# Attention scores in quarter products, gate products moved behind the values, and work exchanged between GpSimd and VectorE

## The chip, the cores and the metric

The kernel runs on one core of one Trainium2 chip. The metric is the device time of one execution in microseconds, the median of the runs. A core has five engines with queues of their own: TensorE (PE in the profile, with its weight loads as PEld), VectorE (DVE), ScalarE (ACT), GpSimd (POOL) and SyncE (SP), which here only issues transfers.

## What is computed

Attention over keys and values that are averaged in groups of eight, and behind it a layer of eight experts. A token takes part in the second if a score says so, and goes to one expert.

```python
# q, k, v: (8, 8, 576, 64); pool = 8, so Sp = 72
k_p = k.reshape(B, H, Sp, pool, D).mean(axis=3)
v_p = v.reshape(B, H, Sp, pool, D).mean(axis=3)
scores = scale * np.matmul(q, k_p.transpose(0, 1, 3, 2))
scores = scores - np.max(scores, axis=-1, keepdims=True)
attn = np.exp(scores)
attn = attn / (np.sum(attn, axis=-1, keepdims=True) + 1e-09)
x = matmul(attn, v_p), as 4608 tokens x 512
# experts
do_compute = x @ w_skip > 0
logits = x[do_compute] @ w_gate                  # 8 experts
e_idx, gate_w = argmax and its softmax weight
h = np.maximum(xc @ w1[e], 0.0)                  # 512 -> 1024
out[do_compute] = xc + gate_w * (h @ w2[e])      # 1024 -> 512; other rows are x itself
```

## The kernel before

Two halves follow each other: attention (`attention`, until about 147 us), then the experts (`experts`). Between them stands the work that turns the routing into lists of tokens (`slots`).

Attention goes over 36 tiles of 128 tokens. A batch has 576 tokens, four and a half tiles, so four tiles straddle two batches. Products on TensorE are fp32; a product of two fp32 operands shows in the profile as two records, each with a weight load. Heads are taken in pairs: `kbd` holds the summed keys of two heads as a block diagonal, 128 rows by 2 x 72 columns, and a query block of 128 rows (two heads of 64) by 128 tokens is the weight side. `scores` (L299) makes the scores of four heads into a bank `sc`, and is called twice for a tile. On a straddling tile each product is made twice, for 64 tokens each (`parts`, L294).

The steps of tile t in the loop from L842, in the order in which the program is written:

- `turned_p` (L326), ScalarE: copies the turned probabilities of tile t-2 out of `pt`, 640 columns in one instruction.
- `normal(t-3)` (L797), VectorE: divides the values of tile t-3 (`rc`, `l8`, `x`), issues the output write on SP, sums the gate logits `lg`, and takes up to two routing steps.
- `scores` of tile t, TensorE; `softmax`, VectorE: the minima `mn` (`least`, L307) of both halves.
- If a batch's gates are due: `gates_pe` (L275, TensorE) here, ahead of the values; `gates_dve` (L280, VectorE) behind the turns.
- `routes.products()`: the ranking products of a routing group (L397 to L401).
- `exponentials`, ScalarE: eight instructions (L315) of 72 columns.
- `values(t-2)` (L331), TensorE: six fp32 products into `o`.
- `turn_p` (L318), TensorE: five turns of tile t-1's exponentials into `pt`.
- VectorE's planned work (`dve.take`), more routing steps up to a budget, GpSimd's planned work (`gps.take`), and, one tile before a batch's gates, `turn_v` (L258).

GpSimd's work is planned by `Spaced` (L640): an item has a first tile, a last tile and a cost; items go in order of their last tile, and writes to the routing table (L415, one indirect DMA a tile) are put between them, at least 1.2 us of other work apart where there is other work. From tile 26 on (`FILLS`) a memset that clears a row block (L768) is put between two writes that have less than 0.5 us between them. Its items are: the sums of a batch's values over eight (`sums`, L241, four large and four small steps), the block-diagonal value operand (`values_both`, L269), the low parts of expert weights (`low`, L584), and the routing table's writes. Expert weights are split into a high part (ScalarE, L581) and a low part, weight minus high part. Of chunks 2 to 6 the second half's low part is made by VectorE (`low_v`, L588), the others by GpSimd; a chunk's place in `stage` is loaded again when both are made. SP issues loads and output writes in program order.

Behind the last tile TensorE works on 56 product steps of one expert (`tile_steps`), in a fixed order; 20 of them are left for the time after the hand-over to `experts`. In between `slots` has GpSimd gather rows of the routing table (L1040) once the last table write has landed, and TensorE turn them (L1072).

## Time and profile before

| | us |
|---|---|
| median of 3 runs | 480.49 |
| lowest and highest | 479.95 and 480.70 |
| profiled execution, its own time | 481.24 |
| its span in the profile | 479.2 |
| granted TensorE clock, mean of the span | 0.999 |

| engine | busy us of the span |
|---|---|
| TensorE (matmul records) | 463.5 (97%) |
| VectorE | 303.4 (63%) |
| GpSimd | 250.3 (52%) |
| ScalarE | 225.7 (47%) |

The shares are averages over two halves that are not alike: VectorE, ScalarE and GpSimd are much busier in the attention half. A busy TensorE is a chain of overlapping records, whose ends are modelled; distances between starts say more than the length of one.

### The profile page before, as it was taken

The numbers are of one execution on the slowest core, as the hardware profiler recorded it, in microseconds if no ns is written. First come the engines' busy times: TensorE is split into PE (matmuls) and PEld (weight loads), VectorE is DVE, ScalarE is ACT, GpSimd is POOL, SyncE is SP. The second block draws the span as 40 slices with busy tenths as digits, with TensorE's granted clock in tenths as the row PEclk, the third lists the DMA queues.
The fourth block names the chain that finished last, engine by engine and source line by source line (L and its number), as shares of the span: only waits on it lengthen the run. The fifth ranks groups of instructions, "written<-read, shape, count | busy, mean of one in ns | idle before, by whom it ended". The sixth has DMA issues, their size and how long they took to land. (4 is left out here: it accounts for less than half of the span.)

```text
span 479.2 us, 11182 instructions
## 1 busy us (share of the span) xinstructions
PE 463.5 (97%) x3043; PEld 417.1 (87%) x3044; DVE 303.4 (63%) x713; ACT 225.7 (47%) x578; POOL 250.3 (52%) x328
## 2 busy tenths in 40 slices
PE   7999999999999999899999999999999999999995
PEld 4799899989999979798989987989899898989894
DVE  5877888798788622578795667663846554343321
ACT  5678768888891211546462645612435251212110
POOL 4499499999998154363342424362624161515242
PEclk9999999999999999999999999999999999999999
DMA  8999999996931026679787497877687223322021
GB/s 278 388 396 390 361 352 332 384 333 207 328 122 68 11 62 215 230 228 308 247 289 244 136 290 241 300 240 251 202 256 262 89 95 101 129 66 88 22 88 42
DMA packets 52042, 103.88 MB, mean 217 GB/s; under 512 B 10031, under 2 KB 22959, under 8 KB 50336
## 3 DMA queue, kind: packets, MB, share of 16 engines
q1 hardware_dynamic: 40544, 78.18, 47.8%
q0 software_dynamic: 11456, 25.22, 15.0%
q8 instruction: 17, 0.28, 0.2%
q14 instruction: 25, 0.20, 0.1%
HBM read 80.85 MB, written 31.21 MB: 234 GB/s over the span
## 5 line engine op out<-in xcount | busy, mean ns | idle before, releaser
L1289 POOL DMA_INDIRECT out<-ring,slot x33 | 35.8, 1085 | 109.3 <-POOLq L1115 105.6
L315 ACT ACTIVATE e<-sc,mn 128x72 f32<-128x72 f32 x288 | 65.0, 345 | 7.4 <-DVE mn L309 6.8
L1527 ACT ACTIVATE hhi<-psl 128x256 fp32r<-128x256 f32 (+3 forms) x59 | 23.5, 400 | 94.0 <-ACTq L1115 93.5
L1384 PE MATMUL psl<-xlo,w1hi 128*128 128x256 f32 (+3 forms) x220 | 64.1, 291 | 0.0
L1383 PE MATMUL psl<-xhi,w1hi 128*128 128x256 f32 (+3 forms) x220 | 64.0, 291 | 0.0
L1385 PE MATMUL psl<-xhi,w1lo 128*128 128x256 f32 (+3 forms) x220 | 64.0, 291 | 0.0
L1284 POOL DMA_INDIRECT ring<-out,slot x42 | 46.6, 1109 | 22.6 <-issue 22.4
L341 PE MATMUL o<-vbd,pT 128*128 128x148 f32 (+1 forms) x312 | 49.4, 298 | 1.1 <-DVE x L360 1.1
L1626 DVE SCALAR_TENSOR_TENSOR hlo<-psl,hhi 128x256 fp32r<-128x256 f32 (+2 forms) x55 | 23.2, 423 | 41.3 <-DVEq L1115 39.0
L415 POOL DMA_INDIRECT table<-pay,r_di x36 | 36.7, 1018 | 12.6 <-DVE mb L443 6.4
L1383 PEld LDWEIGHTS psl<-xhi,w1hi 128*128 128x128 f32 x220 | 41.3, 188 | 0.8 <-issue 0.4
L1384 PEld LDWEIGHTS psl<-xlo,w1hi 128*128 128x128 f32 x220 | 41.3, 188 | 0.5
L341 PEld LDWEIGHTS o<-vbd,pT 128*128 128x128 f32 (+1 forms) x312 | 38.6, 179 | 3.6 <-ACT ring L213 1.0
L1385 PEld LDWEIGHTS psl<-xhi,w1lo 128*128 128x128 f32 x220 | 41.2, 187 | 0.0
L1297 POOL DMA_DIRECT2D sorted<-ring x39 | 22.2, 572 | 32.9 <-DMA ring<-out,slot 25.8
L1603 DVE TENSOR_TENSOR w2lo<-stage,w2hi 128x1024 fp32r<-128x1024 f32 x28 | 34.3, 1223 | 6.6 <-DVEq L1115 6.4
L1384 PE MATMUL psd<-xlo,w1hi 128*128 128x256 f32 (+3 forms) x132 | 38.4, 291 | 0.0
L1385 PE MATMUL psd<-xhi,w1lo 128*128 128x256 f32 (+3 forms) x132 | 38.4, 291 | 0.0
L1383 PE MATMUL psd<-xhi,w1hi 128*128 128x256 f32 (+3 forms) x132 | 38.4, 291 | 0.0
L1409 PE MATMUL mb<-w2hi,hlo 128*128 128x512 f32 x88 | 34.8, 396 | 0.0
L1409 PE MATMUL psf<-w2hi,hlo 128*128 128x512 f32 x88 | 34.8, 396 | 0.0
L1407 PE MATMUL psf<-w2hi,hhi 128*128 128x512 f32 x88 | 34.8, 395 | 0.0
(276 smaller groups left out, 1216.0 us busy)
## 6 DMA issues: line engine op xcount, KB each, us to landing
stage<-in_w SPq DMA_DIRECT2D x64, 512.0 KB, 5.5
sorted<-ring POOLq DMA_DIRECT2D x39, 256.0 KB, 3.3
out<-x SPq DMA_DIRECT2D x36, 256.0 KB, 5.4
stage<-in_k SPq DMA_DIRECT2D x6, 1152.0 KB, 8.8
blocks<-sorted SPq DMA_DIRECT2D x100, 64.0 KB
qt<-in_q SPq DMA_DIRECT2D x9, 512.0 KB, 7.4
hhi<-in_vm SPq DMA_DIRECT2D x4, 1024.0 KB, 7.7
hlo<-in_vm SPq DMA_DIRECT2D x3, 1024.0 KB, 9.8
```

The costliest lines, as they stand in the source:

```text
L315: nc.scalar.activation(ev[:, h // 2, k0:k0 + SP], sc[:, h * SP:(h + 1) * SP], AF.Exp, bias=mn[:, 4 * i + h:4 * i + h + 1], scale=-1.0)
L341: nc.tensor.matmul(o_[sl, g * 2 * VA:(g + 1) * 2 * VA], pT[:, 2 * a + g, sl], vbd[b % 2][:, 2 * a + g, :], start=(g == 0), stop=False)
L415: m = nc.gpsimd.indirect_dma_start(table, bass.IndirectOffsetOnAxis(ap=di[:, j:j + 1], axis=0), flat(fin["pays"][:, t0 + j:t0 + j + TW // ...
L1284: g.indirect_dma_start(ring[:, (s + 3) % 9, 0:D], None, out, bass.IndirectOffsetOnAxis(ap=slot[:, s:s + 1], axis=0), bounds_check=NTOK - 1 ...
L1289: g.indirect_dma_start(out, bass.IndirectOffsetOnAxis(ap=offsets, axis=0), ring[:, (s + 3) % 9, 0:D], None, bounds_check=NTOK - 1, oob_is_ ...
L1383: t.matmul(ps, whi[0][:, k, w], xhi[:, k, xs], start=(k == 0), stop=False)
L1384: t.matmul(ps, whi[0][:, k, w], xlo[:, k, xs], start=False, stop=False)
L1385: last = t.matmul(ps, wlo[0][:, k, w], xhi[:, k, xs], start=False, stop=(k == 3))
L1407: t.matmul(ps, hhi[:, k, sl], whi[1][:, k, :], start=(k == 0), stop=False)
L1409: last = t.matmul(ps, hlo[:, k, sl], whi[1][:, k, :], start=False, stop=(k == 7))
L1527: a.activation(hhi[:, f, xs], bank(f, xs, alone), AF.Relu).then_inc(sem["act"], 1)
L1603: v.tensor_tensor(chunk_of(wlo, c), chunk_view(stage[c], c), chunk_of(whi, c).bitcast(F32), ALU.subtract).then_inc(sem["wlo1" if c < 4 els ...
```

## The change

It does these things:

- From tile 3 on a tile's scores are made in quarters: 64 rows (one head) by 64 tokens, 72 columns, with head parity choosing the bank. The first three tiles stay as they were (`scores_by_halves`). `exped` takes its columns from the banks accordingly.
- The turned probabilities lie in two banks of `pt` (three turns in the first, two in the second), and two copies instead of one take them out. The turned value sums move within `pt`.
- `gates_pe` is written behind the values of its tile; `gates_dve` goes to the next tile, ahead of that tile's scores.
- Routing products that were not yet due when the tile began go behind the values from tile 15 on; after such products a tile takes one more routing step. The two steps for the gate weight come before the two for the rank.
- All low parts of chunks 0 to 6 are planned on GpSimd; chunk 7's stay on VectorE.
- For batches 3, 5 and 7 GpSimd makes two of the four large steps of the value sums, and VectorE sums the four parts that are left in one reduction, ahead of the minima of the tile before the batch's gates. The value operand of these batches may start two tiles later and ends one tile later.

```diff
+FOURS = 3, 5, 7
@@ sums
-            if b:
+            if b and b not in FOURS:
                 first += [add(vt[:, 0:2], vt[:, 0:2], vt[:, 2:4]), add(vs, vt[:, 0], vt[:, 1])]
+        def sum_four(b):
+            nc.vector.tensor_reduce(vss[b], vts[b][0][:, 0:4].rearrange("p i n -> p n i"), axis=AX.X, op=ALU.add)
@@ scores
+        def scores(t):
+            if by_halves(t):
+                return [scores_by_halves(t, i) for i in range(2)]
+            sc = [ps_s.tile([128, 512], F32, name="sc")[:, 0:4 * SP] for _ in range(2)]
+            for g in range(4):
+                for i, sl in enumerate(halves):
+                    b = (t * 128 + i * 64) // S
+                    for r, o in zip(halves, range(2)):
+                        nc.tensor.matmul(sc[o][sl, g * SP:(g + 1) * SP], qts[t // QG][r, t % QG, g, sl],
+                                         kbd[b % 2][r, g, o * SP:(o + 1) * SP], start=True, stop=True)
+            return sc
@@ turned_p
-            pT = ap.tile([128, 5, 128], F32, name="pT")
-            nc.scalar.activation(flat(pT), ptf[:, 0:640], AF.Copy)
+            pT = [ap.tile([128, 3 - i, 128], F32, name=f"pT{i}") for i in range(2)]
+            for i, sl in enumerate((slice(0, 384), slice(256, 512))):
+                nc.scalar.activation(flat(pT[i]), pt[:, i, sl], AF.Copy)
@@ route
-            for a, b in zip(ranked, paid) if last else zip(paid, ranked):
+            for a, b in zip(ranked, paid) if last else (paid, ranked):
@@ later_low
-            if cc > 1 and i:
-                dve.add(now["t"] + 1, now["t"] + 2, 0.65, lambda: low_v(cc, i))
-                return
             gps.add(now["t"] + (2 if cc > 4 else 1), (NT if cc > 5 else wload(cc + 3)) - 1, 1.25, lambda: low(cc, i))
@@ the batches' plan
-            gps.add(t0 - 2 + 3 * slow, t0 - 1 + 2 * slow, 1.25, lambda b=b: values_both(b))
+            four = 2 * (b in FOURS)
+            gps.add(t0 - 2 + 3 * slow + four, t0 - 1 + 2 * slow + four // 2, 1.25, lambda b=b: values_both(b))
@@ the loop over tiles
+            known = routes.held
             routes.exponentials()
             if t > 2:
                 normal(t - 3)
-                sc = [scores(t, i) for i in range(2)]
+                if t - 1 in turns:
+                    gates_dve(turns[t - 1])
+                sc = scores(t)
+            if t + 1 in turns and turns[t + 1] in FOURS:
+                sum_four(turns[t + 1])
...
-            if new is not None:
-                gates_pe(new)
...
-            else:
-                routes.products()
+            elif known or t < PICKED:
+                routes.products()
+            else:
+                routes.exponentials()
             spent = act.take(t, 0.4 if new is not None else 0.0, 1)
             exponentials(t, sc, mn)
             os_[t - 2] = values(t - 2, pts.pop(t - 2))
+            if new is not None:
+                gates_pe(new)
+            fresh = t < NT - 1 and routes.products()
...
-            if new is not None:
-                gates_dve(new)
...
             while t < NT - 1 and busy < (DVE if t < PICKED else DVEL) and routes.step():
-                busy += 0.24
+                busy += 9 if fresh else 0.24
```

## Rows read from the trace of the kernel before

**Rows 1.** Busy us (instructions) of each engine in a stretch; clock, DMA share, GB/s

```profile
56.00:104.00 48.00, 47.69 (x416) 44.95 (x416) 40.12 (x134) 38.82 (x134) 44.90 (x48) 1.00 0.96 344
```

**Rows 2.** Order in time, TensorE, plain tile: start us, us, engine, line, tiles

```profile
82.33 0.27 PE L324 MATMUL pt<-cfs,e 128*128 128x128 f32 x1
82.44 1.15 PE L303 MATMUL sc<-ring,xhi 128*128 128x144 f32 x8
83.50 0.74 PE L341 MATMUL o<-vbd,pT 128*128 128x148 f32 x4
...
85.66 0.53 PE L303 MATMUL sc<-ring,xhi 128*128 128x144 f32 x3
```

**Rows 3.** Waits of GpSimd, 56 to 160 us: total us, times, longest us

```profile
POOL table L415 <- issue: 5.2, 30, 0.3
```

**Rows 4.** Order in time, GpSimd, at the first table write

```profile
55.78 1.08 POOL L415 DMA_INDIRECT table<-pay,r_di  x1 [6.39 <-DVE mb L443]
```

**Rows 5.** Order in time, GpSimd, at the end of the attention half

```profile
152.45 0.99 POOL L415 DMA_INDIRECT table<-pay,r_di  x1 [0.31 <-DVE s_n L1001]
...
155.03 0.98 POOL L415 DMA_INDIRECT table<-pay,r_di  x1 [0.30 <-issue]
158.10 1.08 POOL L1040 DMA_INDIRECT stage<-table,s_coli  x1 [2.08 <-DVE s_last L1060]
```

**Rows 6.** TensorE at L1072: its sequencer's wait (ns, start), then in time

```profile
L1072 PEldq EVENT_SEMAPHORE  x1: 1459/1459/1459, 160.7 to 160.7; - x1
162.82 0.34 PE L1072 MATMUL o<-cfs,stage 81*128 81x81 f32 x2
```

**Rows 7.** Order in time, TensorE, a tile that straddles two batches

```profile
23.22 0.27 PE L324 MATMUL pt<-cfs,e 128*128 128x128 f32 x1
23.42 1.20 PE L303 MATMUL sc<-ring,xhi 128*64 128x144 f32 x16
24.58 0.52 PE L341 MATMUL o<-vbd,pT 128*128 128x148 f32 x2
```

**Rows 8.** Order in time, TensorE, small products of the routing

```profile
91.60 0.26 PE L399 MATMUL mb<-r_oh,ones 128*128 128x40 bf16 x4
91.71 0.18 PE L401 MATMUL mb<-r_oh,upper 128*128 128x32 bf16 x1
```

**Rows 9.** ScalarE: a plain tile in time, then one line (ns min/median/max)

```profile
82.69 0.70 ACT L328 ACTIVATE pT<-pt 128x640 f32<-128x640 f32 x1 [0.28 <-PE pt L324]
83.82 1.80 ACT L315 ACTIVATE e<-sc,mn 128x72 f32<-128x72 f32 x8
...
L267 ACT ACTIVATE vT<-pt x8: 484/484/491, 15.9 to 123.8; 128x384 f32<-128x384 f32 x8
```

**Rows 10.** Waits of TensorE's weight loads, whole span: total us, times, longest us

```profile
PEld mb L278 <- ACT vT L267: 2.2, 5, 0.8
```

**Rows 11.** Order in time, VectorE, tile 25

```profile
102.10 0.74 DVE L208 TENSOR_REDUCE kp<-stage 128x72 f32<-128x576 f32 x1
102.76 1.84 DVE L589 TENSOR_TENSOR w1lo<-stage,w1hi 128x512 fp32r<-128x512 f32 x1
```

**Rows 12.** Groups of GpSimd's instructions, 56 to 156 us: busy us, mean ns

```profile
L768 POOL MEMSET ring<- 128x516 f32 x15 | 8.3, 551 | 0.0
...
L585 POOL TENSOR_TENSOR w1lo<-stage,w1hi 128x512 fp32r<-128x512 f32 x6 | 7.7, 1285 | 0.1
...
L271 POOL TENSOR_TENSOR vbd<-vs,cfs 128x512 f32<-128x512 f32 x4 | 4.2, 1054 | 0.0
...
L248 POOL TENSOR_TENSOR vs<-hlo 128x256 f32<-128x256 f32 x2 | 1.5, 736 | 0.0
```

**Rows 13.** Waits of TensorE, whole span: total us, times, longest us

```profile
PE psf L1394 <- PEq L1115: 1.9, 2, 1.4
```

**Rows 14.** One 512-column product, early and later: ns min/median/max, first and last start

```profile
L739 PE MATMUL o<-ring x6: 1041/1061/1222, 1.7 to 6.2; 128*128 128x512 f32 x6
L817 PE MATMUL o<-ring x6: 592/592/595, 10.9 to 14.8; 128*128 128x512 f32 x6
```

More of the change, by code (lines that the diff above doesn't have):

```diff
@@ L297, in parts, with by_halves, scores_by_halves @@
             return [(slice(0, 128), b0)] if b0 == b1 else [(slice(0, 64), b0), (slice(64, 128), b1)]
[L299 removed]
+        def by_halves(t):
+            return t < 3
+        def scores_by_halves(t, half):
             sc = ps_s.tile([128, 512], F32, name="sc")[:, 0:4 * SP]
             for g in range(2):
[L302 to L304 removed]
+                nc.tensor.matmul(sc[:, g * 2 * SP:(g + 1) * 2 * SP], qts[t // QG][:, t % QG, half * 2 + g],
+                                 kbd[0][:, half * 2 + g, :], start=True, stop=True)
+            return sc
[9 more added lines that the diff above has]
+                                         kbd[b % 2][r, g, o * SP:(o + 1) * SP], start=True, stop=True)
             return sc
@@ L812, in exponentials @@
             es[t] = ebuf[t % 2]
-            for i in range(2):
-                exped(es[t], sc[i], mn, i)
+            for n in range(2):
+                exped(es[t], sc[n], mn, n, by_halves(t))
         def constant_product():
@@ L836, in attention @@
         gates_dve(0)
-        sc = [scores(2, i) for i in range(2)]
+        sc = scores(2)
         mn = softmax(2, sc)
@@ L855, in attention @@
                 normal(t - 3)
-                sc = [scores(t, i) for i in range(2)]
+                if t - 1 in turns:
+                    gates_dve(turns[t - 1])
+                sc = scores(t)
+            if t + 1 in turns and turns[t + 1] in FOURS:
+                sum_four(turns[t + 1])
             if t == NT - 1:
```

35 lines of the change are left out of this document (18 added, 17 removed).

## The prediction

> **What bounds the kernel now.** I read the stretches first (busy time of each engine per stretch), then the order in time of TensorE, then the chain behind the end of the attention half. From 56 to 104 us TensorE is busy 47.69 of 48.00 us, and GpSimd 44.90 [rows 1]. A plain tile takes 85.66 - 82.44 = 3.22 us, with no gap that another engine would have to answer for: eight records of scores, twelve of values, five turns [rows 2]. So TensorE sets the pace of the tiles. The second reading matters more here: GpSimd lacks only 3.1 us of those 48, and the waits say what such gaps are: 5.2 us of issue in thirty gaps of at most 0.3 us before the table writes [rows 3]. After its one long pause, 6.39 us before the first table write at 55.78 us [rows 4], no pause of GpSimd is over 0.31 us until its last table write starts at 155.03 us [rows 5]. It has a queue of its own, about 100 us long, that runs back to back. At the end this queue is on the path: the last table write (until 156.0), the gather of rows (L1040, issued at 158.10) [rows 5], and TensorE's turn of those rows (L1072). TensorE's sequencer stood at L1072 from 160.7 for 1.459 us, until 162.16, and the turn itself began at 162.82 [rows 6]: the queue had about 0.65 us to spare against TensorE. Whatever TensorE gains over 0.65 us in the attention half is lost in front of L1072, unless GpSimd's last table write comes earlier too. The order of instructions around L1072 is fixed when the program is built, so no later product can slip in.
>
> **Scores in quarters (33 tiles, from tile 3 on).** Today a plain tile's four fp32 products show as eight records of 144 columns: (1.15 - 0.28)/7, about 0.12 us apart, 1.06 us from the first score to the first value [rows 2]. The four tiles that straddle two batches already use column halves: sixteen records, 1.16 us to the first value, 0.20 us after the last turn instead of 0.11 [rows 2, 7]. Twice the records in about the same time: two column halves do run side by side, and going into and out of halves costs about 0.19 us (I take 0.25, since the first record of a series is also late). The change makes thirty-two records of 72 columns, four places at a time. If row halves run side by side too, eight steps of 0.12 us become eight of 0.06: -0.49 us, with 0.25 for the switch about -0.25 on each of 29 plain tiles, and -0.49 on the four straddling ones: -9.2 us. No record of before uses a row half, so the bounds are four at a time (0.49 us) and two at a time (0.98 us, +0.25 x 29 = +7 us). In between lies the rate of issue: small bf16 records follow each other at (0.26 - 0.18)/3 = 0.027 us [rows 8], thirty-two of them in 0.86 us. I take four at a time, because the nearest row, the column halves, shows the full effect.
> The Trainium skill (TensorEngine Tiling (Array Packing), Instruction Overhead) puts some 60 cycles on each matmul, however few its columns. By that page 32 x 60 cycles at 2.4 GHz is, as an estimate, 0.80 us a tile, and the quarters would gain nothing on a plain tile; the rival "quarters don't pack" below has this from rows.
>
> **What that meets.** The copy of the turned probabilities takes 0.70 us, and the eight exponentials behind it 1.80 us [rows 9]. Today the scores cover that copy. With half the scores it would end last, and the split into two copies over two banks (the first starts after three turns) takes that away. A copy of 384 columns is 0.484 us [rows 9], so the two end some 0.05 us after the one of today. ScalarE has then 2.5 us of fixed work in a tile of 3.0, and VectorE, busy 40.12 of 48 us [rows 1], 2.7. I take 2 us off TensorE's gain for that crowding (bounds 0 and 6).
>
> **Gates and routing products behind values.** They take waits off the path: TensorE waited 2.2 us in five places for the copy that the gates read [rows 10]. I take -1.4 (bounds -2.2 and 0). The gates' two small VectorE products move ahead of the next tile's minima, some 0.4 us in seven tiles: 0 to +2.9, I take +1, because VectorE has a few tenths spare in a tile.
>
> **Low parts to GpSimd.** VectorE loses five instructions. One of them took 1.84 us [rows 11], more than a tile can hide, so I take -0.8 for it and nothing for the other four (bounds 0 and -1.8). GpSimd gains 5 x 1.285 = +6.4 us [rows 12].
>
> **Sum of four on VectorE (batches 3, 5, 7).** A sum over 576 elements takes 0.74 us [rows 11]; 1024 take 1.32 by proportion, and I take 1.2, since a part of the 0.74 is fixed. It stands ahead of the minima, and minima, exponentials and the next copy wait for it: 0 to 1.2 us in three tiles, I take +0.8 each, +2.4. GpSimd loses one step of 512 columns, as wide as a low part's 1.285 us, and one of 0.736 for each of the three [rows 12].
>
> **TensorE's side in sum:** -9.2 - 1.4 - 0.8 + 2.4 + 1 + 2 = -6.0 us at L1072 (bounds -11 and +6).
>
> **GpSimd's queue in sum.** Between the first and the last table write: +6.4 for the low parts; -4.0 for batches 5 and 7 (batch 3's sums lie ahead of the long pause, so they free nothing); +1.06 because the value product of batch 3 moves behind the pause (its first tile goes from 11 to 13) [rows 12]. From tile 26 on a clearing memset of 0.551 us stands between two table writes that have nothing else between them [rows 12]. Carrying the rule of L649 to L670 through with the new due tiles, four of the fifteen fall away, because low parts and batch 7's value product stand there instead: -2.2. Sum +1.2 us (bounds 0 and +2.5).
> The start: the first write waits for VectorE's routing in tile 12 [rows 4]. Tiles 3 to 11 bring it some 2.0 us earlier; the sum of four for batch 3 stands ahead of that routing on VectorE: +1.2. Net -0.8 (bounds -2.3 and +1.2).
> Last table write: -0.8 + 1.2 = +0.4 us. Less the 0.65 us to spare: -0.2 us. The DMAs stay the same in number; a low part that GpSimd makes later frees its chunk later, and SP, in order, holds output writes behind that chunk's load. Three to four tiles of 3.2 us lie between that load and its use, so I take nothing; without them ScalarE would wait, at most a low part's 1.285 us each time.
> The profiled execution took 481.24 us with a span of 479.2, and lies 0.75 us over the median of 480.49. With -0.2 its span would be 479.0, and the median **480.3 us**.
>
> **Rivals.**
> - *TensorE cools while it waits (slower).* With a lead of 6 us TensorE stands some 5 us in front of L1072. Once warm it stands nowhere so long in the trace; the longest wait is 1.4 us [rows 13], and the granted clock stays at 1.00. The same 512-column product took 1.061 us in the opening series and 0.592 later [rows 14], which is the difference between the two levels, 1.2 and 2.4 GHz, less a fixed part. The slow series started between 1.7 and 6.2 us [rows 14]; as long a stretch at half speed after L1072 costs some 2 us: 482 us. It decides once TensorE's lead over GpSimd is several us.
> The Trainium skill (TensorE: Matmul & The Clock Gate, Part 1) has the clock fall on idleness too; no run here shows it after a warm start.
> - *GpSimd is not the wall.* If its queue shrinks with the tiles (more memsets gone, a start 3 us earlier), TensorE's gain gets through: 474 to 477.5 us. For it: the memsets are only spacing. Against: issue gaps and no waits [rows 3].
> - *Quarters don't pack.* With thirty-two records at 0.027 us a plain tile gets 0.86 + 0.25 - 0.98 = 0.13 us longer, -0.12 on a straddling one: +3.3; with serial row halves +7.3. The other edits give back some 1 us, as a longer tile hides the sum of four: 482.8 to 486.8 us, and TensorE never waits at L1072. Then the change does not do what it says.
> - *GpSimd's lag reaches into the tiles* (a value product too late for its values): some 482 to 484 us. The planner's last tile for a value product lies three tiles, some 9.7 us, ahead of its first values; for batches 3, 5 and 7 the change makes that two.
>
> **How the numbers follow.** Chances: GpSimd's queue ends the gain and the clock holds 0.37 (478.7 to 481.9, at 480.3); with the clock lost 0.26; gain through 0.15; quarters that don't pack 0.14; lag 0.08. A measurement of this kernel can tell about 0.2%, 1 us. Faster: 0.15 + 0.37 x 0.3 + a little = 0.28; within: 0.37 x 0.5 + 0.26 x 0.3 + a little = 0.30; slower: the rest, 0.42. The likeliest case lies near no change, and its own range stands above; for 8 in 10 the range is 475.5 to 484.5.
>
> **What would show it.** Scores: records of 64 rows by 64 columns, and on a plain tile 1.06 us from first score to first value down to about 0.8. If that stays at 1.06 or more, the quarters don't pack. Behind it: a wait of TensorE before L1072 of several us, and the last table write within 1.5 us of 155.03. If that write starts 3 us earlier or more, GpSimd was no wall and the main step is wrong. A sum of four far from 1.2 us, or no late minima in tiles 12, 21 and 30, would show that step wrong.

## The result and the profile after

The changed kernel takes **487.82 us** (median of 4 executions, 485.73 to 488.47) beside 480.6 us of the kernel before on the same chip: ratio 1.0139, 95% interval 1.0108 to 1.0170. It is some 7 us slower, and outside the range of the prediction. The profiled execution took 488.47 us, with a span of 486.2.

The stretches of the kernel after: us, then busy time of each engine (records), and at the end the granted clock of TensorE, the share of the DMA engines and GB/s.

```profile
core 0: us, PE busy (x) PEld busy (x) DVE busy (x) ACT busy (x) POOL busy (x), PEclk, DMA share, GB/s
56.00:86.00 30.00, 27.20 (x454) 24.71 (x454) 25.70 (x91) 24.59 (x92) 27.84 (x30) 1.00 0.96 339
86.00:92.00 6.00, 3.96 (x53) 3.34 (x53) 4.69 (x12) 3.99 (x16) 4.64 (x6) 0.94 1.02 385
92.00:98.00 6.00, 6.00 (x30) 5.74 (x30) 1.73 (x8) 2.26 (x9) 3.31 (x3) 0.50 0.61 236
98.00:102.00 4.00, 4.00 (x46) 3.78 (x46) 2.91 (x11) 2.97 (x11) 3.52 (x4) 0.56 0.54 161
```

From 86 to 92 us TensorE is busy 3.96 of 6.00 us, and behind that its clock stands at the lower of its two levels (0.50, 1.2 GHz) until about 101.5 us. Before, it was busy 47.69 of 48 us over 56 to 104 at a clock of 1.00 [rows 1]. TensorE's order in time there, kernel after (start, us, operation, and in brackets the idle time ahead and who ended it):

```profile
85.20 0.73 PE L321 MATMUL sc<-ring,xhi 64*64 64x72 f32 x32
85.95 0.74 PE L363 MATMUL o<-vbd,pT 128*128 128x148 f32 x4
...
88.33 0.27 PE L266 MATMUL pt<-cfs,ls 128*128 128x128 f32 x1
88.53 0.34 PE L321 MATMUL sc<-ring,xlo 64*64 64x72 f32 x2
89.40 0.34 PE L321 MATMUL sc<-ring,xlo 64*64 64x72 f32 x4 [0.53 <-ACT e L335]
90.71 0.71 PE L321 MATMUL sc<-ring,xlo 64*64 64x72 f32 x26 [0.97 <-ACT ring L214]
91.97 0.65 PE L419 MATMUL mb<-offs,cfs 128*128 128x40 f32 x2 [0.55 <-ACT ex L416]
92.42 0.30 PE L421 MATMUL mb<-r_oh,ones 128*128 128x40 bf16 x4
92.57 0.19 PE L423 MATMUL mb<-r_oh,upper 128*128 128x32 bf16 x1
92.60 1.33 PE L363 MATMUL o<-vbd,pT 128*128 128x148 f32 x4
```

Tile 21 (85.20) shows what the quarters can do: 32 score records, 0.75 us to the first value, where the kernel before took 1.06 [rows 2]. Tile 22 (88.53) shows the loss: its scores stop after two records and again after six. The same four value records then take 1.33 us in place of 0.74, which is the fallen clock. The scores wait for ScalarE, and ScalarE for VectorE; the same microseconds there, kernel after:

```profile
85.12 0.68 DVE L382 TENSOR_TENSOR x<-o,rc 128x512 f32<-128x512 f32 x1
86.01 1.98 DVE L260 TENSOR_REDUCE vs<-hhi 128x256 f32<-128x1024 f32 x1
87.91 0.80 DVE L327 TENSOR_REDUCE mn<-sc 128x4 f32<-128x288 f32 x2
...
88.39 1.81 ACT L335 ACTIVATE e<-sc,mn 128x72 f32<-128x72 f32 x8 [1.94 <-DVE mn L327]
90.22 0.44 ACT L214 ACTIVATE ring<-kp 64x288 f32<-64x288 f32 x1
```

The new sum of four (L260) takes 1.98 us and stands in front of the minima of tile 21. The exponentials (1.81 us) start 1.94 us late, and the keys of the new batch (L214, into `ring`) stand behind them on ScalarE. Only when these keys are done, at 90.66, can tile 22 go on with its scores. So the sum holds not one small step but a chain of four engines' work: sum, minima, exponentials, keys, scores.

From the start of its scores to that of the next, tile 22 takes 9.54 us (4.61 before) and tile 23 takes 4.55 (3.21). The scores of tiles 22 and 23, kernel before, and those of tile 23, kernel after:

```profile
89.29 1.27 PE L303 MATMUL sc<-ring,xlo 128*64 128x144 f32 x16
93.90 1.15 PE L303 MATMUL sc<-ring,xlo 128*128 128x144 f32 x8
...
98.08 1.24 PE L321 MATMUL sc<-ring,xlo 64*64 64x72 f32 x32
```

Tile 35 starts at 144.90 in place of 138.55. At the end, kernel after (GpSimd, then TensorE):

```profile
161.48 0.98 POOL L437 DMA_INDIRECT table<-pay,r_di  x1 [0.31 <-issue]
164.56 1.08 POOL L1068 DMA_INDIRECT stage<-table,s_coli  x1 [2.09 <-DVE s_kind L1087]
...
169.71 0.34 PE L1100 MATMUL o<-cfs,stage 81*128 81x81 f32 x2
```

The last table write starts 6.45 us later than in [rows 5], and the turn of the gathered rows (L1100, L1072 of the kernel before) 6.89 us later than in [rows 6], with no idle time of TensorE's array in front of it. The rest is as long as before: 316.5 us from there, against 316.3. **All of the loss lies in the attention half.** GpSimd is late because the tiles are late. After its long pause it now waits for other engines (engine, line, what it waited for: us in total, times, longest; kernel after):

```profile
POOL table L437 <- DVE l L381: 3.0, 1, 3.0
POOL w2lo L607 <- ACT w2hi L604: 2.5, 3, 1.7
POOL vbd L275 <- DVE vs L260: 0.8, 1, 0.8
```

3.0 + 2.5 + 0.8 = 6.3 us, of the 6.45 by which its last write is late; the first table write starts at 55.79 us, as before. In the kernel before no pause of that kind came behind the first table write [rows 3, 5].

### The profile page after: what moved, and what is told of

Its sections match the earlier page's. It is cut to its first block, busy times and chain, and to the rows that moved or that the text cites. A ratio compares the mean times of both kernels' runs of the same rounds, so it can differ in the third digit from the quotient of the medians.

```text
span 486.2 us, 12741 instructions
## 1 busy us (share of the span) xinstructions
PE 460.4 (95%) x3803; PEld 410.2 (84%) x3804; DVE 302.7 (62%) x711; ACT 227.4 (47%) x614; POOL 247.9 (51%) x323
## 5 line engine op out<-in xcount | busy, mean ns | idle before, releaser
L1312 POOL DMA_INDIRECT ring<-out,slot x42 | 48.8, 1162 | 23.3 <-issue 23.1
L363 PE MATMUL o<-vbd,pT 128*128 128x148 f32 (+1 forms) x312 | 51.6, 306 | 5.0 <-DVE x L382 2.8
L363 PEld LDWEIGHTS o<-vbd,pT 128*128 128x128 f32 (+1 forms) x312 | 40.6, 186 | 8.4 <-ACT pT L350 4.1
L327 DVE TENSOR_REDUCE mn<-sc 128x4 f32<-128x288 f32 x72 | 29.7, 450 | 13.2 <-PE sc L321 8.5
```

The lines of the kernel that those rows point to most:

```text
L327: nc.vector.tensor_reduce(mn[:, i * 4:i * 4 + 4], sc.rearrange("p (h k) -> p h k", k=SP), axis=AX.X, op=ALU.min)
L363: nc.tensor.matmul(o_[sl, g * 2 * VA:(g + 1) * 2 * VA], pT[a][:, g, sl], vbd[b % 2][:, 2 * a + g, :], start=(g == 0), stop=False)
L1312: g.indirect_dma_start(ring[:, (s + 3) % 9, 0:D], None, out, bass.IndirectOffsetOnAxis(ap=slot[:, s:s + 1], axis=0), bounds_check=NTOK - 1 ...
```

## The experiments

The kernel before ran beside every kernel on its chip (medians of 479.6 to 480.6 us). Kernels that did not share a chip are compared by their ratios to it; 0.1% is about 0.48 us. By the intervals of two ratios, their difference is uncertain by some 0.4 to 0.6%; a smaller difference is called not clear below. "Loop" is the time at which the scores of tile 35 start, in one profiled execution: 138.55 before, 144.90 after. The scores of tile 3 start between 19.4 and 21.2 us in these executions, so a difference of 1 us between two loops can come from the start alone. Executions in which the clock fell are longer, so the loop is given with its tiles where it matters.

Three theories stood against each other. Theory 1: the sum of four in front of the minima is the loss, with the clock that it costs. Theory 2: it is the gates and routing products in their new places. Theory 3: it is GpSimd's queue, grown by the low parts.

### Which part costs: five runs with a part undone

**e1: GpSimd makes all sums.**

```diff
-FOURS = 3, 5, 7
+FOURS = ()
```

> The changed kernel, but GpSimd keeps making all four-part value sums; quarters, later gates and the low parts on GpSimd stay. Theory 1 (the sum of four, 1.97 us on VectorE in front of the minima of tiles 12, 21 and 30, holds up the scores of the next tile, and the clock falls for it in tile 22): tiles 13, 22 and 31 take some 3.0 us each, the clock stays near 1 from 86 to 102 us, the attention loop ends about 9 us earlier, and the time is 480 to 483 us, held then by GpSimd's queue, which gets some 4 us longer. Theory 2 (the waits of the routing steps for the gates' products, and the gates' two steps in front of the minima): 486 to 488 us. Theory 3 (GpSimd's queue is the wall in front of the last products, L1072 of the kernel before): no gain at all, 488 to 492 us, the last table write later than in the changed kernel (161.5 us).

Measured: 484.62 us (ratio 1.0093, 1.0056 to 1.0131). The loop is 6.8 us earlier (138.12), and the clock held from 86 to 102. Tiles 13, 22, 23 and 31 take 3.65 + 5.24 + 3.55 + 3.93 = 16.37 us together; in the changed kernel they took 4.89 + 9.54 + 4.55 + 5.65 = 24.63. So three sums of four cost 8.3 us of tile time. At the end only 0.46% (2.2 us) of that came out, which is not clear, and 484.6 us lies between the ranges of theories 1 and 2. The reason stands in front of the turn (TensorE's order of e1, then two of its stretches):

```profile
162.94 0.34 PE L556 MATMUL sc<-xhi,w1lo 128*128 128x384 f32 x1
165.26 0.42 PE L1100 MATMUL o<-cfs,stage 81*128 81x81 f32 x2 [1.98 <-issue]
...
163.00:166.00 3.00, 1.02 (x7) 0.77 (x6) 0.28 (x2) 0.49 (x1) 0.00 (x0) 1.00 0.14 37
166.00:170.00 4.00, 4.00 (x15) 3.78 (x14) 1.63 (x5) 0.49 (x1) 0.00 (x0) 0.57 0.01 4
```

TensorE waits 1.98 us for the rows that follow GpSimd's last table write (157.92), and behind that wait its clock is 0.57. In the tiles theory 1 holds: they were lost with the sum. With it gone TensorE meets the end of GpSimd's queue, as theory 3 has it.

**e2: the sum of four behind the minima.**

```diff
-            if t + 1 in turns and turns[t + 1] in FOURS:
-                sum_four(turns[t + 1])
...
                 mn = softmax(t, sc)
+            if t + 1 in turns and turns[t + 1] in FOURS:
+                sum_four(turns[t + 1])
```

> The changed kernel, with the sum of four behind the minima of its tile instead of in front of them; nothing else moves. Theory 1: what costs is the place, so 480 to 483 us, no fall of the clock in tile 22, tile 13 and 31 under 3.6 us. If the length of the step costs wherever it stands (the routing steps behind it come 2 us later): 484 to 487 us. Theory 2 and theory 3: as the changed kernel, 487 to 488.5 us.

Measured: 482.88 us (1.0058, 1.0028 to 1.0089): 0.81% (3.9 us) less than the changed kernel, by two lines moved. VectorE, then TensorE, of e2:

```profile
86.74 0.82 DVE L327 TENSOR_REDUCE mn<-sc 128x4 f32<-128x288 f32 x2
87.48 1.99 DVE L260 TENSOR_REDUCE vs<-hhi 128x256 f32<-128x1024 f32 x1
...
89.52 0.44 PE L265 MATMUL pt<-cfs,vs 128*128 128x128 f32 x2 [0.55 <-DVE vs L260]
90.00 0.73 PE L321 MATMUL sc<-ring,xlo 64*64 64x72 f32 x32
```

The scores of tile 22 run through (4.75 us), though the turn of the sum itself still waits 0.55 us for it. Two tiles did not get better: tile 13 still takes 4.92 us, where under 3.6 was expected, and tile 24 takes 6.82 (3.44 in the changed kernel). VectorE and TensorE of e2 in tile 24:

```profile
97.83 2.18 DVE L494 TENSOR_TENSOR mb<-offs,cfs 128x8 f32<-128x8 f32 x1
...
101.14 1.13 PE L363 MATMUL o<-vbd,pT 128*64 128x148 f32 x8 [2.10 <-DVE x L382]
```

A subtraction of eight columns, which took 0.17 us in the changed kernel, takes 2.18 here; TensorE stands 2.10 us, and its clock is at half speed from 101.3 to 104.7 us. The sum is not in this chain; e13 follows the step up.

**e3: the quarters alone.** The kernel before with the new scores, exponentials and turned copies; nothing else. Its edit is these parts of the change, cut to the core:

```diff
-            sc = [scores(t, i) for i in range(2)]
+            sc = scores(t)
...
-            pT = ap.tile([128, 5, 128], F32, name="pT")
-            nc.scalar.activation(flat(pT), ptf[:, 0:640], AF.Copy)
+            pT = [ap.tile([128, 3 - i, 128], F32, name=f"pT{i}") for i in range(2)]
+            for i, sl in enumerate((slice(0, 384), slice(256, 512))):
+                nc.scalar.activation(flat(pT[i]), pt[:, i, sl], AF.Copy)
```

> The kernel before with the scores in quarters alone (and the layout of the turned exponentials that goes with them): sums, gates, low parts and routing order as before. By the prediction's own steps the attention loop gains 9.2 us less 2 us of crowding, GpSimd's queue gains 0.8 us, and TensorE waits 4 to 6 us in front of the last products: 479 to 480.3 us if GpSimd's queue is the wall, 473 to 476 us if it is not. If it is crowding that eats the quarters' gain (VectorE and ScalarE cannot follow tiles of 3.0 us): 480 to 483 us with TensorE waiting inside the tiles and not at the end.

Measured: 480.48 us (1.0007, 0.9983 to 1.0032): no change that can be told. Plain tiles take 2.99 to 3.01 us, as forecast, but over tiles 3 to 34 the shorter tiles give only 3.7 us and the longer ones take 5.1 back. In its profiled execution the loop ends at 139.66, later than before. The largest two: tile 5 (+1.85; its clock stood at half speed from 30.7 to 34.1 us) and tile 26 (+0.90). Tile 26, VectorE, GpSimd and TensorE of e3:

```profile
103.19 2.68 DVE L611 TENSOR_TENSOR w1lo<-stage,w1hi 128x512 fp32r<-128x512 f32 x1
...
104.03 1.27 POOL L607 TENSOR_TENSOR w1lo<-stage,w1hi 128x512 fp32r<-128x512 f32 x1
...
107.00 0.74 PE L363 MATMUL o<-vbd,pT 128*128 128x148 f32 x4 [2.33 <-DVE x L382]
```

A low part on VectorE takes 2.68 us here (1.84 in [rows 11]); the normalisation `x` stands behind it, and the next values wait for `x`, since they need the PSUM that it frees.

**e4: gates and routing products where they were.**

```diff
+            if new is not None:
+                gates_pe(new)
             if t > NT - TILES:
                 xlow()
...
-            elif known or t < PICKED:
-                routes.products()
             else:
-                routes.exponentials()
+                routes.products()
...
-            if new is not None:
-                gates_pe(new)
-            fresh = t < NT - 1 and routes.products()
...
+            if new is not None:
+                gates_dve(new)
```

> The changed kernel with the gates' products ahead of the values, the gates' two VectorE steps at the end of their tile and the routing products where the kernel before has them; quarters, sum of four and low parts stay. Theory 2 (routing steps wait for gates' products in the same PSUM tile, 4.2 us in tile 22 and about 1 us in three others, and the gates stand in front of the minima): 3 us or more faster than the changed kernel, 483 to 485 us. Theory 1: at most 1 us faster, 486.8 to 488 us, with the fall of the clock in tile 22 still there.

Measured: 487.7 us (1.0168, 1.0135 to 1.0200): nothing gained. Theory 2 falls as the cause of the loss. By tiles both of its halves are real: the new places save about 0.5 us in tiles 9 and 27 (3.93 us in the changed kernel, 4.46 here), and cost 0.6 in tiles 19 and 29 (3.59 in place of 3.02 and 3.01), where VectorE's routing steps wait for the gates' products (waits of VectorE, changed kernel):

```profile
DVE mb L429 <- PE mb L282: 5.2, 2, 4.2
DVE mb L402 <- PE mb L282: 1.5, 1, 1.5
```

The 4.2 us lie in tile 22, at the fallen clock.

The trace of e4 is of its quickest execution: 483.32 us at a mean clock of 0.994, where the other four took 487.55 to 488.75 at 0.983 to 0.986. In it tile 22 has the same stops (0.54, 0.97, 0.55 us), but the clock stands low only from 92.6 to 96.0 us, against 91.3 to 101.5 in the changed kernel; tiles 22 and 23 take 8.38 and 3.01 us. The longer executions are those with the lower mean clock. But that is not all of the loss: one execution of the changed kernel took 487.75 us at a mean clock of 0.994.

**e7: the diffs of e2 and e4 together.**

> The changed kernel with two things put right: the sum of four behind the minima, and gates and routing products where the kernel before has them. Against the run with the sum behind alone (482.9 us): if the gates and the routing order cost (stalls of 0.6 us each in the tiles behind a routing product, 14, 19, 23, 29, 32, 33, and the 2.3 us in tile 24), 480 to 481.5 us; if the 0.5 us that they give in each of the tiles 5, 9, 27, 31 balances that, 482.5 to 483.5 us.

Measured: 487.58 us (1.0130, 1.0081 to 1.0180), 0.72% (3.5 us) more than e2, which neither reading expected. GpSimd runs the same order in both, but in e7 it waits longer (waits of GpSimd, e7):

```profile
POOL vbd L275 <- DVE r_cm L410: 3.5, 1, 3.5
POOL w1lo L607 <- ACT w1hi L604: 1.6, 1, 1.6
```

In e2 the first is 1.6 us and the second absent, while a wait for a transfer is 0.7 us longer there: 2.8 us more waiting in e7, and its first table write is 0.44 us later. That makes 3.2 us, and the last table write is 3.19 us later (162.44 against 159.25); TensorE waits 2.3 us in front of the turn. A wait anywhere in GpSimd's queue comes out at its end in full. That the two waits come of the gates' place is inferred; the profiled execution of e7 also had its clock at half speed in tile 13.

### The low parts and the sums on their own

**e5: quarters, and all low parts on GpSimd.** e3 with one cut:

```diff
-            if cc > 1 and i:
-                dve.add(now["t"] + 1, now["t"] + 2, 0.65, lambda: low_v(cc, i))
-                return
```

> The kernel before with the quarters and with all early low parts on GpSimd; value sums, gates and routing as before. Against the quarters alone VectorE loses five or six low parts of 1.8 to 2.7 us each, of which the one in tile 26 held the values up by 2.3 us, and GpSimd gains as many of 1.28 us. If VectorE's steps between two tiles' normalisations set the pace: the scores of tile 35 start at 136 to 137.5 us (139.66 in the quarters alone). If GpSimd's queue then is the wall: last table write at 160 us or later, a wait of 2 us or more in front of the turn of the gathered rows, the clock at half speed behind it, and 482 to 485 us in all. If GpSimd is no wall: 477 to 479 us.

Measured: 485.19 us (1.0092, 1.0062 to 1.0123). The loop is 2 us earlier than in e3 (137.62) and the time 0.85% (4.1 us) longer. What TensorE waited for around 160 us in e5:

```profile
PE o L1096 <- issue: 3.5, 1, 3.5
```

Last table write at 159.01, then 3.5 us of waiting and a granted clock of 0.57 in the four microseconds from 167. This is the prediction's wall and its first rival at once, in one part of the change.

**e6: quarters, and the sums of four behind the minima,** low parts and gates as before: e7 with the three lines that e5 cuts still there.

> The kernel before with the quarters and with the sums of four of three batches on VectorE, behind the minima; low parts, gates and routing as before. If VectorE sets the pace: three steps of 1.98 us come on top, the scores of tile 35 start at 140 to 143 us, and the time is 481 to 484 us although GpSimd's queue is 4 us shorter. If GpSimd's queue sets the end: last table write 2 to 4 us earlier than in the quarters alone (156.3 us), and 476 to 479 us.

Measured: 486.06 us (1.0124, 1.0083 to 1.0166), though GpSimd has 4 us less to do. That is slower than either reading expected, and its last table write is even later (158.35 against 156.29 in e3). The loop ends at 141.77. VectorE sets the pace there, so a step taken from GpSimd came back to it as tiles that are late.

### Length against place

**e9: e2, with two adds of contiguous operands.**

```diff
-            nc.vector.tensor_reduce(vss[b], vts[b][0][:, 0:4].rearrange("p i n -> p n i"), axis=AX.X, op=ALU.add)
+            vt = vts[b][0]
+            nc.vector.tensor_tensor(vt[:, 0:2], vt[:, 0:2], vt[:, 2:4], ALU.add)
+            nc.vector.tensor_tensor(vss[b], vt[:, 0], vt[:, 1], ALU.add)
```

> The changed kernel with the sum of four behind the minima and made of two adds of contiguous operands (128x512, then 128x256) instead of one reduction over a stride. If the length of the step is what still costs there (the turns of the value sums wait 0.7 us for it in tiles 21 and 30): some 1.1 us in place of 1.98 us, no such wait, 481 to 482.2 us. If adds of two SBUF operands are stretched beside GpSimd as the low parts are (1.8 to 2.7 us instead of 0.68): no shorter, 482.5 to 484 us.

Measured: **481.41 us** (1.0018, 0.9987 to 1.0049): 1.21% less than the changed kernel, and the loss is gone within what can be told. Against e2 it is 0.40%, which is not clear. The adds take 0.68 and 0.42 us in place of 1.98, and the turns of tile 21 no longer wait.

**e15: the two adds, but still in front of the minima.**

> The changed kernel with the sum of four in its place in front of the minima, but as two adds of 0.68 and 0.43 us instead of one step of 1.98 us. If the length in that place is what costs: the scores of tiles 13, 22 and 31 wait about 0.9 us less, the clock holds in tile 22, and the time is 482 to 484.5 us. If any work in that place breaks the chain from minima to keys: 486 us or more.

Measured: 482.37 us (1.0069, 1.0032 to 1.0105). The shorter step alone, in the same place, recovers about half of the loss (0.70 of 1.39%). Tile 22 takes 5.90 us, at full clock in the profiled execution. In tile 30 the first add took 1.70 us instead of 0.68, and tile 31 still took 5.77.

**e16: the changed kernel, with products without a use ahead of the scores of tiles 13, 22 and 31.**

```diff
+            for _ in range(DUMMIES if turns.get(t) in FOURS else 0):
+                nc.tensor.matmul(sc[0], ident, cfs[:, 0:4 * SP], start=True, stop=True)
             for g in range(4):
```

> The changed kernel with eight products without a use (128x288 each) ahead of the scores of tiles 13, 22 and 31, where TensorE waits for keys. If the fall of TensorE's clock is a large part of what tile 22 costs (9.54 and 4.55 us for tiles 22 and 23, against 8.38 and 3.01 in the run with the gates as before whose clock fell for 3.4 us): the clock holds from 86 to 102 us, tile 22 takes 5 to 6.5 us, and the time is 482.5 to 485 us. If the waiting itself is the cost: no change, or 1 to 2 us slower by the added products.

Measured: 491.68 us (1.0235, 1.0216 to 1.0254). The eight products take about 4 us, twice what I meant them to, so the time, which lies in neither expected range, says little; the tiles say more (TensorE and a stretch of e16):

```profile
91.40 4.05 PE L319 MATMUL sc<-cfs 128*128 128x288 f32 x16
95.38 0.73 PE L324 MATMUL sc<-ring,xlo 64*64 64x72 f32 x32
...
92.00:98.00 6.00, 6.00 (x66) 4.91 (x65) 2.63 (x8) 4.63 (x18) 5.62 (x6) 1.00 0.93 341
```

With TensorE busy through the wait the clock stays at 1.00, tile 22 takes 3.96 us from its scores on, and tile 23 takes 3.56. Of what tiles 22 and 23 took in the changed kernel I estimate the clock's share thus: the pieces of tile 22, each as long as in tiles at full clock (scores with their stops 2.66, routing 1.16, values with the step behind them 1.60, gates 0.58, turns with the step behind them 0.74) make 6.74 us against 9.54, and tile 23 takes 3.56 against 4.55: 2.8 + 1.0 = 3.8 us of the 14.09. That is an estimate for one execution, since no run held the clock without another change.

### What stands still beside GpSimd

**e13: e9, and one small step of tile 24 reads the counts from PSUM.**

```diff
-                yield from near_tokens(offs)
+                yield from near_tokens(fin["counts"])
```

> The run with two adds behind the minima (481.4 us), and one VectorE step in tile 24 (128x8, a subtraction of counts, 0.2 us long by its size but 1.96 us in that run) reads the counts from PSUM instead of their copy in SBUF. If it stood still because both operands were in SBUF while GpSimd added: it takes 0.2 us, tile 24 falls from 5.05 to 3.4 us or less, and the scores of tile 35 come some 1.6 us earlier. If it waited for something else: no change of its 2 us. Of the 1.6 us the end sees nothing if GpSimd's queue is the wall (a wait of 1 to 2 us in front of the turn, 480.5 to 482 us), all of it if not (479.5 us).

In e9 tile 24 takes 5.05 us. VectorE, GpSimd and TensorE of e9:

```profile
96.70 1.96 DVE L496 TENSOR_TENSOR mb<-offs,cfs 128x8 f32<-128x8 f32 x1
...
96.66 0.74 POOL L249 TENSOR_TENSOR vl<-vl 96x256 f32<-96x256 f32 x1
97.35 1.28 POOL L249 TENSOR_TENSOR hlo<-hlo 128x512 f32<-128x512 f32 x1
...
99.79 0.47 PE L365 MATMUL o<-vbd,pT 128*64 128x148 f32 x4 [1.87 <-DVE x L384]
```

A subtraction of eight columns takes 1.96 us and ends 0.03 us behind GpSimd's two adds (97.35 + 1.28 = 98.63). The same places of e13:

```profile
96.38 0.16 DVE L496 TENSOR_TENSOR mb<-mb,cfs 128x8 f32<-128x8 f32 x1
...
96.46 0.75 POOL L249 TENSOR_TENSOR vl<-vl 96x256 f32<-96x256 f32 x1
97.14 1.28 POOL L249 TENSOR_TENSOR hlo<-hlo 128x512 f32<-128x512 f32 x1
```

With one operand in PSUM it takes 0.16 us, and tile 24 takes 3.44. In e13 it also started 0.08 us ahead of the adds, so this pair alone leaves a doubt; but the other PSUM steps (the next two, 0.21 and 0.15 us) ran at their usual length beside those adds. The other traces leave less doubt. With both operands in SBUF the same subtraction took 0.17 or 0.18 us wherever no add of GpSimd ran beside it (kernel before, kernel after, e6, e7). Where one did, it ended 0.04 to 0.06 us behind the end of an add, however long that took: 0.37 us in e3, 0.51 in e5, 1.48 in e1, 2.18 in e2. The same picture explains the low parts: [rows 11] starts with GpSimd's low part (102.76, 1.28 us), stands for it, and then takes its own 0.56 us. It explains the 1.70 us in e15 too (118.64 to 120.34, beside a GpSimd low part that ended at 119.77).

The time: 483.02 us (1.0069, 1.0046 to 1.0092). Tile 24's 1.6 us did not reach the end: last table write 156.41, against 157.09 in e9, and a wait of 0.10 us in front of the turn. That is neither of the two times that I expected. It is even 0.51% more than e9, barely clear, and I can't say from these runs why.

### Looking for a kernel that beats both

**e10: e9, gates behind the values only where the tile has no routing product.**

```diff
+            ahead = new is not None and bool(known)
+            if ahead:
+                gates_pe(new)
...
-            if new is not None:
+            if new is not None and not ahead:
                 gates_pe(new)
...
+            if ahead:
+                gates_dve(new)
```

The routing products go back to where the kernel before has them. This kernel is called the mix below.

> The changed kernel with the sum of four as two adds behind the minima, the gates' products behind the values only in the batch tiles whose tile has no routing product, and the routing products where the kernel before has them. If the stalls of 0.6 us in tiles 14, 19, 23, 29, 32 and 33 and the 1.6 us in tile 24 come of routing steps that wait for gates' products in their PSUM tile, they go: scores of tile 35 at 135 to 136.5 us (139.3 us with the two adds alone). GpSimd's queue: if it is the wall, its last table write stays at 156 to 157 us, TensorE waits 1.5 to 3 us in front of the turn of the gathered rows, and the time is 480 to 482 us. If it is no wall: 476.5 to 478.5 us.

Measured: 483.58 us (1.0072, 1.0038 to 1.0105), slower than either reading expected. In the profiled execution (480.53 us, one of the quicker ones) the loop ends at 138.24, not at 136.5 or earlier. The stalls in 19, 23 and 29 went (3.02, 3.01, 3.01 us); tile 24 met the same standing step (2.67 us), tile 32 a new wait, and TensorE waited 0.84 us in front of the turn.

**e11, e12, e14: GpSimd's memsets between late table writes cut to three,** on e10, on e1 and on e13.

```diff
-            nc.gpsimd.memset(bufs["ring"][:, cleared[-1]], 0.0)
+            if len(cleared) <= 3:
+                nc.gpsimd.memset(bufs["ring"][:, cleared[-1]], 0.0)
```

> As the mix, and GpSimd's memsets that stand between its late table writes cut to the first three (the rest clear again what is already clear; the writes then follow each other by the 1.29 us of the last three instead of 1.70). If GpSimd's queue is the wall: last table write 3 to 4 us earlier (153 us), the wait in front of the turn gone, 477 to 479 us. If the writes themselves then wait for their transfers, or if GpSimd is no wall: the same time as the mix.

> The run without sums of four (484.6 us; TensorE waited 1.98 us in front of the turn, and its clock fell to half there) with the same memsets of GpSimd left out, and nothing else: a test of the wall alone. If GpSimd's queue is the wall: last table write at 154 to 155 us in place of 157.9, no wait, no fall of the clock at 166 us, and 481 to 482.5 us. If not: 484 to 485.5 us.

> As the run before, with GpSimd's memsets between the late table writes cut to three. If GpSimd's queue is the wall there: last table write 2 to 4 us earlier than in that run, no wait in front of the turn, 478 to 480 us. If the memsets' place matters in another way (the mix lost 5 us with them gone, its clock at half speed from 127.8 and 148.3 us): 484 us or more, with such falls again.

Measured: 488.68 us (1.0188, 1.0163 to 1.0214), 483.28 us (1.0065, 1.0043 to 1.0086) and 486.4 us (1.0140, 1.0083 to 1.0197). On e1 it does part of what a wall demands: last table write 156.49 in place of 157.92, no wait in front of the turn, no fall of the clock behind it. But the turn itself starts no earlier (165.95, against 165.26 in e1), because TensorE now comes later; only the time behind it is shorter (316.0 against 317.4 us). The 0.28% (1.3 us) in all are not clear. GpSimd could not use all of the room, as it then waited 2.2 us for VectorE. On the other two it costs 0.7 to 1.2% (3 to 6 us): TensorE is busy only 3.75 of the 7 us from 140 to 147 in e14 (6.48 in e13), and the clock falls behind that. Why the tiles stall with the memsets gone stays open.

**The mix with less fill and six sums of four.**

```diff
-FOURS = 3, 5, 7
+FOURS = 2, 3, 4, 5, 6, 7
```

> The mix with fewer memsets, and the two adds on VectorE for six batches (2 to 7) instead of three. GpSimd loses 2 us of sums for each of the other three batches, VectorE gains 1.1 us in each. If GpSimd's queue still sets the end in the mix with fewer memsets: 2 to 4 us faster than it, 474 to 477 us. If VectorE's steps set it: two adds in three more tiles, 0.3 to 1 us each, and 478 to 481 us.

Measured: 490.89 us median, with executions from 482.96 to 492.01, too far apart for a ratio.

**e17: quarters and the gates' mix, sums and low parts as before. e18: the same with one sum of four (tile 21) as two adds, and the PSUM operand.** Their edits are those of e3 and e10 (without sums on VectorE); e18 adds the two adds of e9 with `FOURS = (5,)` and the line of e13.

> The quarters alone (480.5 us), with the gates' products behind the values in the batch tiles that have no routing product; sums, low parts and routing order as in the kernel before. The loop gains 0.5 us in each of tiles 5, 9, 13, 27 and 31, and the wait in tile 5, in which the clock fell in the quarters alone, goes. GpSimd's queue as the wall: first table write about 1 us earlier than in the kernel before (it follows the routing of tile 12), last one 154 us, TensorE waits 1 us or more in front of the turn, 478.5 to 480 us. No wall: 476 to 478 us.

> As the run before, with the sum of four of one batch (tile 21) as two adds on VectorE behind the minima, and the counts of tile 24 read from PSUM. GpSimd's queue is 2 us shorter, VectorE's 1.1 us longer in one tile. GpSimd as the wall: last table write 1.5 to 2 us earlier than in the run before, no wait in front of the turn, 477 to 478.5 us. VectorE as the pace: 0.5 to 1 us slower than the run before.

Measured: 479.09 us (0.9992, 0.9967 to 1.0016) and 481.81 us (1.0051, 1.0025 to 1.0076). e17 is the best of the study and can't be told from the kernel before: its quickest four executions took 477.49 to 478.04 us, at a mean clock of 0.995 to 1.0 (the quickest four of the kernel before, out of 23, took 478.19 to 479.11). Its trace is of a long execution (485.43 us), so whether TensorE waits in front of the turn in the quick ones is not shown. e18 is 0.59% slower than e17, near the second of its two readings. In its trace the last table write came early (154.49), yet TensorE reached the turn at 162.75, as in the kernel before, and did not wait: relieving GpSimd alone gave nothing.

## Why the prediction was wrong, point by point

- **Sum of four: the step that failed, and the cause of the loss.** Forecast 1.2 us long and +0.8 in each of three tiles, +2.4 in all. It is 1.98 us long (the proportion to the 0.74 us of [rows 11] did not hold for four parts read over a stride), and three of them cost 8.3 us of tile time (e1). I followed it to minima, exponentials and copy, and left out the keys of the new batch, which stand behind the exponentials on ScalarE and which the next scores need: 9.54 us in tile 22. Moved behind the minima it cost 3.9 us less (e2), and as two adds there the whole loss was within 0.5% (e9). Against the forecast the term is short by 8.3 - 2.4 = 5.9 us.
- **The clock.** I had it fall in front of the last products, by a wait of several us. In the changed kernel it fell in tile 22, after stops of 0.53, 0.97 and 0.55 us within four microseconds. The rival itself was sound in part: in e1 and e5 the clock stood at 0.57 behind waits of 1.98 and 3.46 us in front of the turn; in e7 it held behind one of 2.34. The Trainium skill (TensorE: Matmul & The Clock Gate, Part 1) has it fall on idleness. These runs agree in that the falls in the changed kernel, e1, e2, e4 and e5 came behind stops of TensorE; e7 shows that a stop is not always followed by one.
- **Quarters pack: right.** A plain tile takes 2.99 to 3.01 us (forecast 3.0), the straddling tiles did not get the 0.49. Small records can follow each other faster than the 0.027 us that I read off [rows 8]: 32 in 0.51 us, 0.016 each. By the estimate from the overhead per matmul of the Trainium skill (TensorEngine Tiling (Array Packing), Instruction Overhead) they would have taken 0.80 us; the trace decides against it. The rival "quarters don't pack" was wrong.
- **Crowding: the other step that failed, mis-sized by as much or more.** I took 2 us off 9.2. Alone, the quarters gave nothing that can be told (e3). The gain shows in the plain tiles and is lost where VectorE or ScalarE end last: batch tiles, tile 12, and every place where a long VectorE step stands between two normalisations. The bound of 6 was too low as well. Without its sum of four the prediction has TensorE gain 6.0 + 2.4 = 8.4 us; in e1, which has no sum of four, tiles 3 to 34 take only 0.3 us less than in the kernel before (tile 5 alone took 1.5 us longer there than in the changed kernel). So this side is short by 6 to 8 us. By these figures, each from one execution, I estimate that either mistake alone would have left the time within the range (TensorE 6.9 us late at the turn, less 5.9, or less 6 to 8); it took both. That e9 ends near the forecast of 480.3 us is luck: its tiles give 0.7 us in place of 8.4, so TensorE reaches the turn just as GpSimd's rows do (a wait of 0.04 us), and not some 5 us ahead of them.
- **Gates and routing behind values: a wash.** Forecast -1.4 and +1. e4 shows no difference that is clear; the half that I missed is that the routing steps write the same PSUM tile as the gates' products and wait for them (the rows under e4).
- **Low parts: the price on GpSimd was right in kind, the gain too small.** Forecast -0.8 on the tiles; tile 26 alone lost 2.3 us of waiting (5.64 in e3, 3.33 in e5; 4.74 in the kernel before). From e3 to e5 GpSimd's queue between first and last table write grew by 4.4 us (99.2 to 103.6), where I had +6.4.
- **GpSimd's queue as the wall: right as a mechanism, wrong as the forecast.** Four kernels waited there (e1 1.98 us, e5 3.46, e7 2.34, e10 0.84), the others 0.1 us or not at all. In the changed kernel TensorE came later than GpSimd, so the likeliest case never arose. I also took the queue's length as a sum of its own steps, +1.2 us. From the first to the last table write it grew by 6.4 us, and 6.3 of them are waits for engines that were late.
- **The bounds of TensorE's side.** I gave -11 and +6 at the turn without showing how they follow; added up, the bounds of the terms reach further both ways. The turn came 6.89 us later.

What is measured, then: of 1.39%, 0.81 go with the place of the sum (e2), and 1.21 with place and length together (e9); the 0.18 that are left are less than can be told. The length alone takes 0.70 in the old place (e15). Behind the minima its share (0.40) is not clear, and part of it is tile 24, which took 6.82 us in e2 and 5.05 in e9 by a step that is not the sum's. How the share of tile 22 divides into waiting and clock is an estimate (e16).

## What to carry to other kernels

Before work is moved into an engine's queue, follow everything that stands behind the new place, on that engine and on the next two, to the first thing that TensorE needs; here the place right behind the step that others wait for cost 3.9 us less than the one in front of it. A gain per tile counts only where TensorE ends last: look at the slack of each other engine in that tile before multiplying by the number of tiles. A queue that runs back to back can be a wall for its length and still grow by the lateness of others.

## What the runs showed of the hardware

- A VectorE step with both inputs in SBUF stood still while GpSimd ran adds of two SBUF inputs, and ended within 0.06 us of the last of them, plus its own work: an 8-column subtraction took up to 2.67 us (e10), against 0.17 or 0.18 with no add beside it and 0.16 with one input in PSUM (e13); a 512-column low part took up to 3.17 (e17), against 0.68. In e10 the subtraction had already stood 0.67 us beside a table write when the first add began, while in other runs such a write did not hold it; that stays open. The sum of four as a reduction (one input) always took 1.97 to 1.99 us. The Trainium skill (SBUF — State Buffer, SBUF: two separate sides) says that the two engines share a pair of ports under an exclusive lock, and that whoever starts first keeps it for the whole instruction. The runs agree, the other way round too: in e17 a low part on GpSimd that started 0.02 us behind one on VectorE took 1.80 us, against 1.28. They add one thing: in e9 the step did not get in between GpSimd's two adds, of which the second starts 0.05 us ahead of the end of the first; it waited for both. It is not always so: in the kernel before a low part at 114.69 us ended 0.55 us behind the first of two adds, and the second took 0.78 us instead of 0.32.
- A reduction over four parts with a stride between them ran at 1.98 us for 1024 elements a partition; two contiguous adds did the same in 0.68 + 0.42.
- Scores of 64 x 64 by 72 columns run four at a time: 32 records start within 0.51 us.
- Several short stops of TensorE (0.5 to 1 us each) were followed by a fall of its clock, which lasted until about 101.5 us in the changed kernel. Behind the same stops it lasted from 92.6 to 96.0 us in the profiled execution of e4; the place of the falls in executions without a trace is not known.
